# Giving out the last network's input sums earlier, and letting late weights' remainders run on two engines: one fused attention, mixture and two-layer kernel on one Trainium2 core

## The chip, the cores and the metric

The kernel runs on one core of a Trainium2 chip (trn2). The metric is device time of one execution in microseconds (us), the median of several. TensorE does the matrix products and transposes, VectorE, ScalarE and GpSimd the elementwise work, SyncE issues transfers. The profile calls them PE, DVE, ACT, POOL and SP; PEld is TensorE's weight load.

## The reference

Three stages run one after the other; all arrays are float32.

```python
# 1. attention, B=2, H=8, S=576, D=64, window 128, a linear bias by distance
attn = softmax(where(mask, q @ k.T * scale + bias, -1e9)) @ v
x = attn.transpose(0, 2, 1, 3).reshape(1152, 512)
# 2. four experts, F=1024, weighted by p = domain_probs / sum
out = sum(p[:, e:e+1] * (relu(x @ w1[e]) @ w2[e]) for e in range(4))
# 3. the last network, 512 -> 2048 -> 512
h = relu(out @ w_in)
y = (h * h) @ w_out
```

## The kernel before, in words

Each float32 operand of a product is split into a rounded high part and the remainder (low part), and three products (high by high, high by low, low by high) are accumulated. The high part is a copy on ScalarE, the remainder a subtraction on VectorE or GpSimd (`rest`, L499 to L501).

The last network is handled as two more experts, so that `e` runs from 0 to 5: 0 to 3 are the experts of stage 2, 4 and 5 the two halves of the 2048 wide hidden layer (in the code `E` is 4). For `e` from 1 on the work is a list of items `(e, ch, g)`: `ch` is one of two groups of tokens (`PAIRS`: four tiles of 128 tokens, and five), `g` one of four quarters of the 1024 hidden columns. An item has two parts. `gemm1_pair` (L1052) computes the first product of the item by a Strassen-like form of seven products of sums, 42 matmuls into three PSUM tiles (`hps`), in the order b11, t2, t1, b21, t3, b22, m4. `flush_one` (L1364) then runs the second product (`gemm2_pair`) of the item before, six matmuls for each token tile into PSUM tiles `yacc`, and at every second `g` empties them (`evac`, L1178). So TensorE's stream is product one of item n, product two of item n-1, product one of item n+1, and so on.

The sums in the first product are of two kinds. Those of the weights are made in `w_forms` (L339): four sums (`wsum`, `add`), roundings on ScalarE (`ha`, `hs`), remainders (`la`, `ls`), fifteen steps on GpSimd with the four remainders (`wl`, `w_ops`, `lo`) of the matching second weight. Those of the inputs are t1, t2, t3 and m4 (high parts `ht`, `hm`, low parts `lt`, `lm`). For the last network the inputs are the outputs of stage 2, so they are made at the turn from `e` = 3 to `e` = 4: `to_x2` (L1204) transposes the finished tiles `ytile` in pairs ("twins") on TensorE into PSUM tiles `xtp` (which share the five `yacc` slots), copies parts with ScalarE and puts a list of steps into `x2bg`: `st1`, `st2`, `sm4`, `st3`, `la` and `lb` read `xtp` in PSUM on VectorE, `hi` (ScalarE) and `lo` (VectorE or GpSimd) make the high parts and remainders. There are three pairs for `ch` = 1 (the last of a single tile) and two for `ch` = 0. The items around the turn are (3,1,2), (3,1,3), (3,0,2), (3,0,3), (4,1,0), (4,1,1), (4,0,0), (4,0,1).

What sets the order of these background steps is `fill` (L1436). It is called after each small piece of TensorE work with the time that piece takes, advances a model clock, and gives out steps whose inputs the model says are ready and whose engine the model says has room (`room`, `by`, `spare`). `x2_run` (L1303) gives out steps of `x2bg` in list order. `x2_need` (L1290) forces those of a sum just before its product. `convert` (L225) is another such list: it turns the last network's weights, which arrive as 64-bit numbers, into float32, with two half tiles in flight; four steps of VectorE (L279, L286, L293 twice) for each half. An engine executes its instructions in the order in which they were given out; an instruction that waits holds those behind it.

Lines named below: L357 `wsum` sums, L501 remainders, L1067 first product, L1078 copies p1 and p5 (ScalarE), L1082 sums u2, u3, c12, c21, c22 (VectorE), L1097 and L1092 square and relu, L1098 and L1102 high part of the hidden values, L1103 their low part for experts, L1147 second product, L1193 and L1199 emptying `yacc`, L1223 transposes, L1236 copies out of `xtp` and high parts, L1240 sums out of `xtp`.

```python
1247            end["b"] = copied(xh[:, 2:4, cb], b[:, 2:4, :], short)
1267                eng = "POOL" if clock["POOL"] <= max(clock["DVE"], clock["now"]) + 0.3 else "DVE"
1305        for _ in range(4):
1447            if conv and need and not (xbg or x2bg or x2todo) and conv_due[0] >= 1.0 and conv[0]() is not False:
```

Of the kernel before, what the change touches and what calls it, by code (L numbers as in the profile page):

```python
# [131 lines left out]
def kernel(  # L132
# [201 lines left out]

    def by(end, early=0.5):

        return clock["force"] or end <= clock["now"] + early

    def w_forms(i):  # L339
# [14 lines left out]
        def add(o, x, y, op):  # L354
            if not room("POOL"):
                return False
            nc.gpsimd.tensor_tensor(out=t["s"][:, o:o + 2, :], in0=x(), in1=y(), op=op)  # L357
            t["end"] = spent("POOL", 0.85)
# [11 lines left out]
        def part_lo(o, src):  # L370
            if not room("POOL"):
                return False
            js = slice(o, o + 2)
            rest("POOL", t["la"][0][:, js, :], src, t["ha"][0][:, js, :])
            spent("POOL", 0.85)
# [8 lines left out]
        def done(o):  # L384
            if not (by(t["hs", o // 4 * 4]) and room("POOL")):
                return False
            if o == 0:
                free.insert(0, buf)
                t["ls"] = w_tile([P, 8, P], F32R, "ls")
            js = slice(o, o + 2)  # L390
            rest("POOL", t["ls"][0][:, js, :], t["s"][:, js, :], t["hs"][0][:, js, :])
            spent("POOL", 0.85)
            if o == 6:
                w1t[e, g] = [t[x] for x in ("ha", "hs", "la", "ls")]
                free.append(t["buf"])
                ready.add(i)
# [15 lines left out]
    def w_ops(i):  # L412
# [24 lines left out]
        def lo(o):  # L437
            if not (by(held["end"]) and room("POOL")):
                return False
            cs = slice(o, o + 2 * P)  # L440
            rest("POOL", flat(held[0][1])[:, cs], raw[:, cs], flat(held[0][0])[:, cs])
            spent("POOL", 0.85)
# [609 lines left out]
    def gemm1_pair(e, ch, g):  # L1052
# [60 lines left out]
        mm(pb, s2, "t2", True, False)  # L1113
        add(u2, pb, p1)
# [8 lines left out]
        mm(pb, s3, "t3", False, False)  # L1123
        add(u3, pb, p1)
# [4 lines left out]
        mm(pc, s4, "b22", False, True)  # L1129
        add(c12, pc, u2)  # L1130
# [73 lines left out]
    def to_x2(ch, tiles):  # L1204
# [58 lines left out]
        def lo(name):  # L1263
            def go():
                if "h" + name not in end or not by(end["h" + name], 0.4):
                    return False
                eng = "POOL" if clock["POOL"] <= max(clock["DVE"], clock["now"]) + 0.3 else "DVE"
                if not room(eng):
# [5 lines left out]
        x2bg.extend([  # L1274
# [3 lines left out]
            hi("t2"),  # L1278
            hi("t1"),
            step("sm4", short, "st2", lambda us: minus(s["m4"], a[:, 2:4, :], s["t2"], us)),  # L1280
            step("st3", short, "b", lambda us: minus(s["t3"], b[:, 2:4, :], s["t3"], us)),
            hi("m4"),
            step("lb", short, "b", lambda us: minus(xl[:, 2:4, cb], b[:, 2:4, :], f32(xh[:, 2:4, cb]), us)),
            hi("t3"),
            lo("t2"), lo("t1"), lo("t3"), lo("m4"),
        ])

    x2made, x2bg = [], []
# [75 lines left out]
    def flush_one():  # L1364
# [5 lines left out]
        turning = (e, f) == (E - 1, NQ - 1)  # L1370
# [4 lines left out]
        if turning:  # L1375
# [3 lines left out]
        for i, tile_ in enumerate(tiles):  # L1379
# [56 lines left out]
    def fill(share, us, need=0.0):  # L1436
# [9 lines left out]
        for _ in range(3):  # L1446
            if conv and need and not (xbg or x2bg or x2todo) and conv_due[0] >= 1.0 and conv[0]() is not False:
# [354 lines left out]
    for it, (e, ch, f, two) in list(enumerate(items))[N1:]:  # L1802
# [69 lines left out]
```

## Time and profile before

| what | value |
| --- | --- |
| three timed runs | 677.43, 677.45, 680.63 us; median 677.45 |
| the profiled execution | 679.51 us, of which the span from first to last instruction is 677.70 |
| mean granted TensorE clock | 0.995 |
| busy: PE | 657.7 us (97%) |
| busy: DVE, POOL, ACT | 476.6, 412.4, 320.4 us |

The busy shares are means over the whole span. A stall of TensorE stands in the profile as idle time ahead of an instruction, with the engine that ended it; granted clock is given for each stretch as a share of full speed. "x3" in a row of the timeline means that three like instructions were merged into one line.

### The profile page before, as it was taken

To read this page: it belongs to the slowest core of one execution; us is meant where nothing else is said; L and a number is where in the kernel's file an instruction comes from. 1 tells how busy PE (TensorE), PEld (TensorE's weight loads), DVE (VectorE), ACT (ScalarE), POOL (GpSimd) and SP (SyncE) were. 2 spreads that over 40 slices of the span, in tenths; PEclk is the share of its full clock that TensorE was granted. 3 is DMA by queue.
4 is the path that set the end of the run, shared out by engine and by line. 5 is a ranking of instruction groups with operands and counts; after the bars stand their busy time and mean duration, and the time that the engine had idled before them with its cause. 6 is when DMAs were issued, how large, how long until landed. Compare 5 with 4: busy or idle time off the path is not lost.

```text
span 677.7 us, 11173 instructions
## 1 busy us (share of the span) xinstructions
PE 657.7 (97%) x3947; PEld 586.0 (86%) x3947; DVE 476.6 (70%) x1037; ACT 320.4 (47%) x802; POOL 412.4 (61%) x506
## 2 busy tenths in 40 slices
PE   9999999999999999999999999996989999899997
PEld 8879988899898989898998988885879898798896
DVE  6898977648888876877777777765675666445553
ACT  6998877514443343434343443453444543333220
POOL 1799967438686554557546435535566667688421
PEclk9999999999999999999999999999999999899999
DMA  9942221023214244343434343311114233000012
GB/s 239 259 139 74 74 82 40 1 63 118 100 61 135 100 135 145 111 139 116 139 115 144 125 144 111 104 48 46 63 47 156 77 95 110 0 1 1 1 63 77
DMA packets 44023, 64.44 MB, mean 95 GB/s; under 512 B 4160, under 2 KB 26176, under 8 KB 43968
## 3 DMA queue, kind: packets, MB, share of 16 engines
q1 hardware_dynamic: 32704, 39.35, 18.8%
q10 hardware_dynamic: 11264, 24.38, 11.3%
q8 instruction: 31, 0.51, 0.3%
q14 instruction: 24, 0.20, 0.1%
HBM read 52.97 MB, written 10.75 MB: 94 GB/s over the span
## 4 chain that ended last, share of the span: by engine, by line
PE 74%; POOL 13%; issue 6%; DVE 4%; ACT 2%; DMA 1%; ACTq 0%; POOLq 0%; DVEq 0%
PE yacc L1147 27%; PE hps L1067 24%; PE yacc L1173 6%; PE hps L950 6%; POOL hmem L501 4%; PE xps L735 3%; PE tp L871 2%; POOL wl L501 2%; PE sc L815 2%; POOL ls L501 2%; POOL wsum L357 1%; POOL la L501 1%; PE sc L525 1%; PE hps L1683 1%; DVE wconv L293 1%
## 5 line engine op out<-in xcount | busy, mean ns | idle before, releaser
L1147 PE MATMUL yacc<-wh,hmem 128*128 128x512 f32 x720 | 230.7, 392 | 3.7 <-DVE y L1240 3.7
L1147 PEld LDWEIGHTS yacc<-wh,hmem 128*128 128x128 f32 x720 | 136.0, 189 | 32.0 <-issue 4.5
L1147 PE MATMUL yacc<-wl,hmem 128*128 128x512 f32 x360 | 141.1, 392 | 0.0
L501 POOL TENSOR_TENSOR wl<-wraw,wh 128x256 fp32r<-128x256 f32 (+1 forms) x91 | 85.5, 964 | 36.4 <-ACT wh L434 22.0
L501 POOL TENSOR_TENSOR hmem<-c,hmem 128x320 fp32r<-128x320 f32 (+1 forms) x64 | 59.4, 941 | 64.9 <-ACT hmem L1098 64.8
L501 POOL TENSOR_TENSOR ls<-wsum,hs 128x256 fp32r<-128x256 f32 x80 | 64.4, 831 | 54.8 <-ACT hs L381 54.0
L1082 DVE TENSOR_TENSOR u<-hps,p 128x256 f32<-128x256 f32 (+1 forms) x80 | 36.5, 456 | 85.1 <-PE hps L1067 72.2
L1078 ACT ACTIVATE p<-hps 128x256 f32<-128x256 f32 (+1 forms) x80 | 32.8, 411 | 110.1 <-PE hps L1067 110.0
L1147 PEld LDWEIGHTS yacc<-wl,hmem 128*128 128x128 f32 x360 | 68.0, 189 | 12.7
L501 POOL TENSOR_TENSOR la<-wraw,ha 128x256 fp32r<-128x256 f32 x60 | 52.5, 898 | 27.1 <-ACT ha L367 27.1
L293 DVE SCALAR_TENSOR_TENSOR wconv<-wraw,wconv 128x512 int32<-128x512 int32 x64 | 56.8, 887 | 1.3
L1102 ACT ACTIVATE hmem<-c 128x256 fp32r<-128x256 f32 (+1 forms) x72 | 31.2, 445 | 53.1 <-DVE c L1082 51.5
L1098 ACT ACTIVATE hmem<-c 128x320 fp32r<-128x320 f32 (+1 forms) x64 | 27.3, 446 | 57.9 <-DVE c L1092 38.4
L1067 PE MATMUL hps<-ht,ls 128*128 128x320 f32 (+1 forms) x160 | 48.1, 301 | 2.5 <-POOL ls L501 2.5
L1103 DVE SCALAR_TENSOR_TENSOR hmem<-c,hmem 128x256 fp32r<-128x256 f32 (+1 forms) x72 | 40.2, 577 | 14.3 <-ACT hmem L1102 12.9
L1067 PE MATMUL hps<-ht,hs 128*128 128x320 f32 (+1 forms) x160 | 48.0, 300 | 0.8 <-ACT ht L1236 0.8
L1067 PE MATMUL hps<-lt,hs 128*128 128x320 f32 (+1 forms) x160 | 47.9, 299 | 0.6 <-POOL lt L501 0.6
L1067 PE MATMUL hps<-xh,ha 128*128 128x320 f32 (+1 forms) x160 | 47.7, 298 | 0.3 <-ACT p L1078 0.3
L1067 PE MATMUL hps<-xh,hs 128*128 128x320 f32 (+1 forms) x160 | 47.6, 297 | 0.5 <-DVE u L1082 0.4
L1067 PE MATMUL hps<-xh,la 128*128 128x320 f32 (+1 forms) x160 | 47.6, 297 | 0.4 <-POOL la L501 0.4
L1067 PE MATMUL hps<-xl,hs 128*128 128x320 f32 (+1 forms) x160 | 47.5, 297 | 0.0
L1067 PE MATMUL hps<-xl,ha 128*128 128x320 f32 (+1 forms) x160 | 47.4, 297 | 0.0
(148 smaller groups left out, 1723.1 us busy)
## 6 DMA issues: line engine op xcount, KB each, us to landing
wraw<-in_w_dram SPq DMA_DIRECT2D x32, 512.0 KB, 4.1
wraw<-in_w_out_dram ACTq DMA_DIRECT2D x16, 512.0 KB, 3.8
w<-wconv ACTq DMA_DIRECT2D x32, 256.0 KB, 3.9
wraw<-w SPq DMA_DIRECT2D x16, 512.0 KB, 3.3
wraw<-in_w_in_dram ACTq DMA_DIRECT2D x14, 512.0 KB, 3.7
rq<-in_qT_dram SPq DMA_DIRECT2D x8, 256.0 KB, 7.2
out_dram<-y SPq DMA_DIRECT2D x8, 256.0 KB, 2.1
rk<-in_kT_dram SPq DMA_DIRECT2D x8, 192.0 KB, 5.2
```

The lines of the kernel that those rows point to most:

```text
L293: nc.vector.scalar_tensor_tensor(out=ai, in0=raw[j][:, :, part], scalar=amount, in1=ai, op0=op, op1=ALU.bitwise_or,)
L501: e.tensor_tensor(out=out, in0=in0, in1=f32(in1), op=ALU.subtract)
L735: nc.tensor.matmul(out=xps[:, :, o0:o0 + w], lhsT=l_, rhs=r_, start=(i == 0 and l_ is wh_ and r_ is hi), stop=(i == len(mm) - 1 and l_ is ...
L950: nc.tensor.matmul(out=ps, lhsT=l_[:, k, cs], rhs=r_[:, k, cols], start=(k == 0 and r_ is xh and l_ is wh and not second), stop=(k == KT - ...
L1067: nc.tensor.matmul(out=ps, lhsT=a[l_][:, k, :], rhs=b[r_][:, k, :], start=start and k == 0 and l_ == r_, stop=stop and k == 1 and l_ == 1, ...
L1078: nc.scalar.activation(out=out, in_=x, func=ACTF.Copy)
L1082: nc.vector.tensor_tensor(out=out, in0=x, in1=y, op=ALU.add)
L1098: nc.scalar.activation(out=hh, in_=r, func=ACTF.Copy)
L1102: nc.scalar.activation(out=hh, in_=src, func=ACTF.Relu)
L1103: nc.vector.scalar_tensor_tensor(out=hl, in0=src, scalar=0.0, in1=f32(hh), op0=ALU.max, op1=ALU.subtract)
L1147: nc.tensor.matmul(out=y, lhsT=l_[:, ns], rhs=r_[:, fo, :], start=(first and fo == 0 and j == 0), stop=(last and fo == FTQ - 1 and j == 2),)
L1173: nc.tensor.matmul(out=y, lhsT=l_[:, ns], rhs=r_[:, fo, :], start=(first and j == 0), stop=(last and j == 2),)
```

## The change

It changes the order and the engine of background steps. No step is added or left out, and TensorE's instructions and SyncE's stand in the same order as before.

1. `x2_run` is called at more places: in `gemm1_pair` ahead of the sums u2, u3 and c12, and in `flush_one` ahead of `evac`; with a slack for VectorE's modelled backlog (`x2_slack`), and up to eight steps instead of four.
2. In `x2bg` the steps that read PSUM (`reads`) stand ahead of the roundings and remainders of all pairs that are still waiting.
3. `lo` chooses GpSimd only if its model clock is 0.4 behind, instead of up to 0.3 ahead.
4. `turning` is true during items (3,0,2), (3,0,3), (4,1,0) and (4,1,1). In these no step of `convert` is given out.
5. `side` lets a weight step of the last network go to VectorE if GpSimd has no room, `x2bg` is empty, `turning` is false and `spare` finds room. All of `add`, `part_lo`, `done` and `lo` use it.

```diff
+    def side(i):
+        if room("POOL"):
+            spent("POOL", 0.85)
+            return "POOL"
+        if order[i][0] >= E and not (x2bg or turning[0]) and spare(0.45):
+            return "DVE"
...
         def add(o, x, y, op):
-            if not room("POOL"):
+            if not by(t.get("end", 0.0), 1.0):
                 return False
-            nc.gpsimd.tensor_tensor(out=t["s"][:, o:o + 2, :], in0=x(), in1=y(), op=op)
-            t["end"] = spent("POOL", 0.85)
+            eng = side(i)
+            if eng is None:
+                return False
+            e_ = nc.gpsimd if eng == "POOL" else nc.vector
+            e_.tensor_tensor(out=t["s"][:, o:o + 2, :], in0=x(), in1=y(), op=op)
+            t["end"] = clock[eng]
...
         def part_lo(o, src):
-            if not room("POOL"):
+            eng = side(i)
+            if eng is None:
                 return False
             js = slice(o, o + 2)
-            rest("POOL", t["la"][0][:, js, :], src, t["ha"][0][:, js, :])
-            spent("POOL", 0.85)
+            rest(eng, t["la"][0][:, js, :], src, t["ha"][0][:, js, :])
...
         mm(pb, s2, "t2", True, False)
+        x2_run(0.9)
         add(u2, pb, p1)
...
         mm(pb, s3, "t3", False, False)
+        x2_run(0.9)
         add(u3, pb, p1)
...
         mm(pc, s4, "b22", False, True)
+        x2_run(0.7)
         add(c12, pc, u2)
...
-                if need not in end or not (room("DVE", 1.0) and by(end[need], 0.4)):
+                if need not in end or not (room("DVE", x2_slack[0]) and by(end[need], 0.4)):
...
-                eng = "POOL" if clock["POOL"] <= max(clock["DVE"], clock["now"]) + 0.3 else "DVE"
-                if not room(eng):
+                eng = "POOL" if clock["POOL"] <= max(clock["DVE"], clock["now"]) - 0.4 else "DVE"
+                if not room(eng, x2_slack[0] if eng == "DVE" else 1.2):
...
-        x2bg.extend([
+        reads = [
             step("st1", short, "a", lambda us: minus(s["t1"], b[:, 0:2, :], s["t1"], us)),
             step("la", 2 * short, "a", lambda us: minus(xl[:, :, ca], a, f32(xh[:, :, ca]), us)),
             step("st2", short, "st1", lambda us: minus(s["t2"], b[:, 2:4, :], s["t1"], us)),
-            hi("t2"),
-            hi("t1"),
+            step("st3", short, "b", lambda us: minus(s["t3"], b[:, 2:4, :], s["t3"], us)),
             step("sm4", short, "st2", lambda us: minus(s["m4"], a[:, 2:4, :], s["t2"], us)),
-            step("st3", short, "b", lambda us: minus(s["t3"], b[:, 2:4, :], s["t3"], us)),
-            hi("m4"),
             step("lb", short, "b", lambda us: minus(xl[:, 2:4, cb], b[:, 2:4, :], f32(xh[:, 2:4, cb]), us)),
-            hi("t3"),
-            lo("t2"), lo("t1"), lo("t3"), lo("m4"),
-        ])
+        ]
+        i = sum(x[0][0] not in "hl" or x[0] in ("la", "lb") for x in x2bg)
+        x2bg[i:i] = reads
+        x2bg.extend(k(x) for x in ("t2", "t1", "t3", "m4") for k in (hi, lo))
...
-    def x2_run():
+    def x2_run(slack=1.0):
-        for _ in range(4):
+        x2_slack[0] = slack
+        for _ in range(8):
...
             if last:
+                x2_run(1.1)
                 evac(e, ch, [tile_], f, two)
...
-            if conv and need and not (xbg or x2bg or x2todo) and conv_due[0] >= 1.0 and conv[0]() is not False:
+            if conv and need and not (xbg or x2bg or turning[0]) and conv_due[0] >= 1.0 and conv[0]() is not False:
...
+        turning[0] = (e, ch, f // 2) in ((E - 1, 0, 1), (E, 1, 0))
```

In `done` and in the `lo` of `w_ops` the engine is chosen in the same way as in `part_lo`. The rows that follow are instructions in the order of the program, without times; the numbers in the names count tiles. Line numbers of the changed kernel are higher by up to 18.

Place one is VectorE in item (3,0,2), from the steps ahead of its sum u2 to its sum u3 (`hps_5135` is the PSUM tile that also takes t3 and m4). Before:

```order
L279 TENSOR_SCALAR wconv_2389<-wconv_2389 128x512
L286 TENSOR_SCALAR wconv_2389<-wconv_2389 128x512
L293 SCALAR_TENSOR_TENSOR wconv_2389<-wraw64_2387,wconv_2389 128x512 x2
L1082 TENSOR_TENSOR u2_5129<-hps_5135,p1_5127 128x256
L279 TENSOR_SCALAR wconv_2389<-wconv_2389 128x512
L286 TENSOR_SCALAR wconv_2389<-wconv_2389 128x512
L293 SCALAR_TENSOR_TENSOR wconv_2389<-wraw64_2388,wconv_2389 128x512
L1103 SCALAR_TENSOR_TENSOR hmem_109<-hps_5134,hmem_109 128x256
L1082 TENSOR_TENSOR u3_5130<-hps_5135,p1_5127 128x256
```

Now:

```order
L513 TENSOR_TENSOR ls_5058<-wsum_4959,hs_4957 128x256
L279 TENSOR_SCALAR wconv_2389<-wconv_2389 128x512
L286 TENSOR_SCALAR wconv_2389<-wconv_2389 128x512
L293 SCALAR_TENSOR_TENSOR wconv_2389<-wraw64_2387,wconv_2389 128x512 x2
L1094 TENSOR_TENSOR u2_5129<-hps_5135,p1_5127 128x256
L1115 SCALAR_TENSOR_TENSOR hmem_109<-hps_5134,hmem_109 128x256
L1094 TENSOR_TENSOR u3_5130<-hps_5135,p1_5127 128x256
L1094 TENSOR_TENSOR c12_5131<-hps_5136,u2_5129 128x256
```

Three steps of `convert` between u2 and the low part of the hidden values are gone from there. Ahead of u2 there is now one remainder `ls` of a weight.

Place two is VectorE in item (4,1,0), the first of the last network, around its sum u2 (`y_2505` is the tile of the third, single pair; `lt21`, `lt11`, `lm41` and `xl` are remainders of t2, t1, m4 and t3 for `ch` = 1). Before:

```order
L1240 TENSOR_TENSOR y_2505<-xtp_5313,y_2505 128x128
L501 TENSOR_TENSOR lt21_5237<-y_2505,ht21_5236 128x2x64
L1082 TENSOR_TENSOR u2_5433<-hps_5439,p1_5431 128x320
L501 TENSOR_TENSOR lm41_5239<-y_2510,hm41_5238 128x2x128
L1240 TENSOR_TENSOR y_2505<-xtp_5313,y_2505 128x128 x2
L1240 TENSOR_TENSOR xl_84<-xtp_5313,xh_83 128x2x64
L501 TENSOR_TENSOR xl_84<-y_2505,xh_83 128x2x64
L1082 TENSOR_TENSOR u3_5434<-hps_5439,p1_5431 128x320
```

Now:

```order
L1255 TENSOR_TENSOR xl_84<-xtp_5310,xh_83 128x4x64
L1255 TENSOR_TENSOR y_2505<-xtp_5310,y_2505 128x128 x3
L1255 TENSOR_TENSOR xl_84<-xtp_5310,xh_83 128x2x64
L513 TENSOR_TENSOR xl_84<-y_2510,xh_83 128x2x128
L513 TENSOR_TENSOR lt21_5232<-y_2505,ht21_5231 128x2x64
L1094 TENSOR_TENSOR u2_5436<-hps_5442,p1_5434 128x320
L513 TENSOR_TENSOR lt11_5230<-y_2505,ht11_5229 128x2x64
L513 TENSOR_TENSOR xl_84<-y_2505,xh_83 128x2x64
L513 TENSOR_TENSOR lm41_5234<-y_2505,hm41_5233 128x2x64
L1094 TENSOR_TENSOR u3_5437<-hps_5442,p1_5434 128x320
```

The reads of `xtp_5310` now all stand ahead of u2. The remainders of t1 and of m4 for the third pair, which GpSimd made, now stand on VectorE behind u2.

Place three is GpSimd ahead of item (5,0,1): sums, remainders `la` and remainders `ls` of its weights, among the remainders of the hidden values (`hmem`) of item (5,0,0). Before:

```order
L501 TENSOR_TENSOR hmem_109<-c22_6488,hmem_109 128x256
L357 TENSOR_TENSOR wsum_6518<-wraw_6119 128x256
L501 TENSOR_TENSOR hmem_109<-c12_6486,hmem_109 128x256
L501 TENSOR_TENSOR hmem_109<-c21_6487,hmem_109 128x256
L501 TENSOR_TENSOR hmem_109<-c22_6488,hmem_109 128x256
L357 TENSOR_TENSOR wsum_6518<-wsum_6518,wraw_6119 128x256
L357 TENSOR_TENSOR wsum_6518<-wraw_6119 128x256
L357 TENSOR_TENSOR wsum_6518<-wraw_6119,wsum_6518 128x256
L501 TENSOR_TENSOR la_6517<-wraw_6119,ha_6515 128x256 x3
L501 TENSOR_TENSOR ls_6608<-wsum_6518,hs_6516 128x256 x4
```

Now:

```order
L513 TENSOR_TENSOR wl_6356<-wraw_5952,wh_6355 128x256 x2
L369 TENSOR_TENSOR wsum_6462<-wsum_6462,wraw_6115 128x256
L369 TENSOR_TENSOR wsum_6462<-wraw_6115 128x256
L513 TENSOR_TENSOR hmem_109<-c22_6497,hmem_109 128x256
L513 TENSOR_TENSOR hmem_109<-c12_6495,hmem_109 128x256
L369 TENSOR_TENSOR wsum_6462<-wraw_6115,wsum_6462 128x256
L513 TENSOR_TENSOR hmem_109<-c21_6496,hmem_109 128x256
L513 TENSOR_TENSOR hmem_109<-c22_6497,hmem_109 128x256
L513 TENSOR_TENSOR la_6461<-wraw_6115,ha_6459 128x256
L513 TENSOR_TENSOR ls_6587<-wsum_6462,hs_6460 128x256 x4
```

Between the last `hmem` step and the first `ls` step there stood three sums and three `la` steps; now one `la` step stands there. One of the sums and two `la` steps went to VectorE. Over the whole kernel VectorE makes 17 of the weight steps that GpSimd made (7 `wl`, 4 `ls`, 4 `la`, 2 `wsum`).

## Rows read from the trace of the kernel before

**Rows 1.** Part 1 of the page: busy us, share of the span, instructions.

```profile
PE 657.7 (97%) x3947; PEld 586.0 (86%) x3947; DVE 476.6 (70%) x1037; ACT 320.4 (47%) x802; POOL 412.4 (61%) x506
```

**Rows 2.** Waits of PE: line, released by, us in total, times, longest us.

```profile
PE yacc L1147 <- DVE y L1240: 3.7, 2, 2.2
PE hps L1067 <- POOL ls L501: 2.5, 2, 1.9
PE hps L1067 <- POOL lm L501: 2.1, 1, 2.1
```

**Rows 3.** Windows: busy us of PE, PEld, DVE, ACT, POOL; granted clock, DMA share, GB/s.

```profile
430.00:500.00 70.00, 61.10 (x347) 52.79 (x346) 45.98 (x94) 31.00 (x82) 38.72 (x49) 0.98 0.19 64
500.00:630.00 130.00, 126.71 (x738) 113.99 (x737) 75.92 (x137) 54.23 (x122) 95.64 (x122) 0.99 0.19 62
...
474.00:478.00 4.00, 4.00 (x12) 3.10 (x12) 2.36 (x5) 0.87 (x2) 2.57 (x4) 0.61 0.33 122
...
584.00:588.00 4.00, 4.00 (x27) 4.00 (x26) 0.84 (x3) 0.77 (x2) 0.64 (x1) 0.70 0.00 0
```

**Rows 4.** Timeline of PE: start us, us, what, idle before it and its releaser.

```profile
439.65 0.38 PE L1067 MATMUL hps<-hm,ha 128*128 128x256 f32 x1 [1.16 <-DVE u L1082]
...
460.52 0.47 PE L1147 MATMUL yacc<-wh,hmem 128*128 128x512 f32 x1 [2.21 <-DVE y L1240]
...
463.36 0.30 PE L1067 MATMUL hps<-xh,ha 128*128 128x320 f32 x1
...
465.18 0.41 PE L1067 MATMUL hps<-ht,hs 128*128 128x320 f32 x1 [0.79 <-ACT ht L1236]
...
472.87 0.42 PE L1067 MATMUL hps<-lm,ha 128*128 128x320 f32 x1 [2.09 <-POOL lm L501]
...
473.71 0.59 PE L1147 MATMUL yacc<-wh,hmem 128*128 128x512 f32 x1
...
494.50 0.47 PE L1147 MATMUL yacc<-wh,hmem 128*128 128x512 f32 x1 [1.54 <-DVE y L1240]
...
499.64 0.38 PE L1067 MATMUL hps<-lt,hs 128*128 128x256 f32 x1 [0.59 <-POOL lt L501]
...
533.27 0.39 PE L1067 MATMUL hps<-ht,ls 128*128 128x256 f32 x1 [0.62 <-POOL ls L501]
...
580.44 0.39 PE L1067 MATMUL hps<-xh,la 128*128 128x256 f32 x1 [0.37 <-POOL la L501]
...
583.31 0.58 PE L1067 MATMUL hps<-ht,ls 128*128 128x256 f32 x1 [1.90 <-POOL ls L501]
```

**Rows 5.** Chain that ended last: start us, us, an undisturbed first product.

```profile
241.95 6.15 PE hps L1067 x42
```

**Rows 6.** Timeline of DVE, columns as in rows 4, at the turn.

```profile
437.82 1.11 DVE L293 SCALAR_TENSOR_TENSOR wconv<-wraw,wconv 128x512 int32<-128x512 int32 x1
...
456.82 1.83 DVE L1103 SCALAR_TENSOR_TENSOR hmem<-c,hmem 128x256 fp32r<-128x256 f32 x2
...
459.51 1.20 DVE L1240 TENSOR_TENSOR y<-xtp,y 128x256 f32<-128x256 f32 x3
...
465.16 0.29 DVE L501 TENSOR_TENSOR lt<-y,ht 128x128 fp32r<-128x128 f32 x1 [3.40 <-ACT ht L1236]
466.61 0.49 DVE L1082 TENSOR_TENSOR u<-hps,p 128x320 f32<-128x320 f32 x1 [1.15 <-PE hps L1067]
...
492.22 0.41 DVE L501 TENSOR_TENSOR lm<-y,hm 128x256 fp32r<-128x256 f32 x1
...
494.93 0.92 DVE L501 TENSOR_TENSOR lt<-y,ht 128x256 fp32r<-128x256 f32 x1
```

**Rows 7.** Timeline of POOL, columns as in rows 4.

```profile
472.37 0.45 POOL L501 TENSOR_TENSOR lm<-y,hm 128x128 fp32r<-128x128 f32 x1
...
579.66 2.11 POOL L501 TENSOR_TENSOR la<-wraw,ha 128x256 fp32r<-128x256 f32 x3
...
581.85 2.79 POOL L501 TENSOR_TENSOR ls<-wsum,hs 128x256 fp32r<-128x256 f32 x4
```

More of the change, by code (lines that the diff above doesn't have):

```diff
@@ L384, in done @@
         def done(o):
-            if not (by(t["hs", o // 4 * 4]) and room("POOL")):
+            eng = side(i) if by(t["hs", o // 4 * 4]) else None
+            if eng is None:
                 return False
@@ L390, in done @@
             js = slice(o, o + 2)
-            rest("POOL", t["ls"][0][:, js, :], t["s"][:, js, :], t["hs"][0][:, js, :])
-            spent("POOL", 0.85)
+            rest(eng, t["ls"][0][:, js, :], t["s"][:, js, :], t["hs"][0][:, js, :])
             if o == 6:
@@ L437, in lo @@
         def lo(o):
-            if not (by(held["end"]) and room("POOL")):
+            eng = side(i) if by(held["end"]) else None
+            if eng is None:
                 return False
             cs = slice(o, o + 2 * P)
-            rest("POOL", flat(held[0][1])[:, cs], raw[:, cs], flat(held[0][0])[:, cs])
-            spent("POOL", 0.85)
+            rest(eng, flat(held[0][1])[:, cs], raw[:, cs], flat(held[0][0])[:, cs])
             if o == 2 * n - 2 * P:
@@ L1277, in to_x2 @@
             step("st2", short, "st1", lambda us: minus(s["t2"], b[:, 2:4, :], s["t1"], us)),
-            hi("t2"),
-            hi("t1"),
+            step("st3", short, "b", lambda us: minus(s["t3"], b[:, 2:4, :], s["t3"], us)),
             step("sm4", short, "st2", lambda us: minus(s["m4"], a[:, 2:4, :], s["t2"], us)),
-            step("st3", short, "b", lambda us: minus(s["t3"], b[:, 2:4, :], s["t3"], us)),
-            hi("m4"),
             step("lb", short, "b", lambda us: minus(xl[:, 2:4, cb], b[:, 2:4, :], f32(xh[:, 2:4, cb]), us)),
-            hi("t3"),
-            lo("t2"), lo("t1"), lo("t3"), lo("m4"),
-        ])
-    x2made, x2bg = [], []
+        ]
+        i = sum(x[0][0] not in "hl" or x[0] in ("la", "lb") for x in x2bg)
+        x2bg[i:i] = reads
+        x2bg.extend(k(x) for x in ("t2", "t1", "t3", "m4") for k in (hi, lo))
+    x2made, x2bg, turning = [], [], [False]
     def x2_need(name):
@@ L1301, in x2_need @@
         clock["force"] = False
-    def x2_run():
-        for _ in range(4):
+    x2_slack = [1.0]
+    def x2_run(slack=1.0):
+        x2_slack[0] = slack
+        for _ in range(8):
             for i, step in enumerate(x2bg):
@@ L1369, in flush_one @@
             first, last = f == 0, f == FT - 1
-        turning = (e, f) == (E - 1, NQ - 1)
+        ending = (e, f) == (E - 1, NQ - 1)
         if first:
@@ L1374, in flush_one @@
         tiles = ys[e, ch]
-        if turning:
+        if ending:
             c0 = PAIRS[ch][0] // P
@@ L1384, in flush_one @@
             if last:
+                x2_run(1.1)
                 evac(e, ch, [tile_], f, two)
-            if turning and i in (2, 4):
+            if ending and i in (2, 4):
                 run_x2()
```

## The prediction

> **What bounds the kernel now.** I read the busy times first: PE works 657.7 of 677.70 us [rows 1], so what can be won by another order of background steps is PE's idle time, some 20 us, and no more. Next comes the windows view [rows 3]: from 430 to 500 us PE is busy for 61.10 of 70 us, so 8.9 us of the idle time lie at the turn into the last network; from 500 to 630 it is idle for another 3.3 us. VectorE is busy for 45.98 and 75.92 us in these stretches, so it has room; what it does in front of a step that PE waits for matters, not its sum. Third, the waits of PE by releaser [rows 2]: VectorE's sums out of `xtp`, GpSimd's weight remainders `ls` and one `lm` lead. Last, the timeline gives each wait its place [rows 4]. Six of the nine waits there belong to the turn, three to weights that come late (533 to 583 us).
>
> A wait can cost more than itself. From 474 to 478 us, behind the wait that ends at 472.87, the granted clock is 0.61 with PE busy throughout; from 584 to 588 us, behind the one that ends at 583.31, it is 0.70 [rows 3, 4]. Full speed is the 2.4 GHz level, so a part of each stretch ran at 1.2 GHz. The first cost (1 - 0.61) x 4 = 1.56 us, the second 1.2 us. The mean of 0.98 over 430 to 500 us gives 1.4 us lost, about the same as that one stretch: the longer wait that ends at 460.52 cost no clock.
>
> **The turn, step by step.** TensorE's order is unchanged, so I go along its waits.
>
> *Item (3,0,2).* PE waits 1.16 us for u3, because steps of `convert` stand between u2 and u3; the last of them ran for 1.11 us from 437.82 [rows 4, 6]. Place one shows that they are gone. The `ls` step that now stands ahead of u2 costs 0.4 to 0.9 us there (below) and is covered by VectorE's wait for u2's product. Saved: 1.16.
>
> *Item (3,0,3).* Five reads now stand between its u2 and the low part ahead of u3, one of them a wide one, where four stood. A read takes 0.4 (1.20 for three [rows 6]), a wide one up to twice that. I charge 0.4, with 0 and 0.8 as ends, since some of it lies beside ScalarE's work for the same low part. Lost: 0.4.
>
> *Product two of (3,0,2).* Its third tile waits 2.21 us for a `yacc` slot that is still an `xtp` tile; the slot is free when `sm4` of the second pair has read it. Those reads start only when VectorE is through two slow `hmem` steps (1.83 from 456.82 [rows 6]). Before, four reads with a wide one came first up to and with `sm4`, about 1.9 us; now `st1` and the wide `la` are done earlier and three come, 1.2 us. The two `hmem` steps stay in front. Saved: 0.6, with 0 and 2.2 as ends.
>
> *Item (4,1,0).* Its first product runs from 463.36 to 473.71 [rows 4], 10.35 us, where the same 42 matmuls take 6.15 undisturbed [rows 5]: 4.2 us too long, of which two waits are 0.79 (for `ht` of the third pair) and 2.09 (for `lm`, which ran 0.45 us on GpSimd from 472.37, behind an `hmem` step [rows 7]). Place two shows both pulled ahead: the reads of the third pair, its `xl` and `lt21` stand ahead of u2, and `lm41` stands on VectorE. But `lt11`, which t1 needs from its second matmul on, stands behind u2, and u2 waits for the end of t2. This makes a new wait: u2 0.49, then `lt` 0.29 [rows 6], and the latency of two hand-overs, less one matmul of 0.15: about 0.9 us. Saved: 4.2 - 0.9 = 3.3, with 2.0 and 4.0 as ends.
>
> *The clock behind it.* With 2.09 us of waiting gone and at most 1.5 us in one piece left, I take the stretch from 474 as run at full speed: saved 1.56, or nothing, if the waits that are left bring the lower level all the same.
>
> *Product two of (4,1,0).* The 1.54 us ahead of 494.50 are a `yacc` slot again, and `sm4` again. After the last slow steps of the item VectorE did `lm` and `st1` (0.41 each, pitch 0.33), `la`, `st2` and `sm4`; now `la`, `st2`, `st3`, `sm4`. Saved: 0.3.
>
> *Item (4,0,0).* PE waits 0.59 us for `lt`, made by GpSimd between weight steps [rows 4]. The step is now on VectorE ahead of u2 and no longer behind weight steps. Saved: 0.59.
>
> The turn in sum: 1.16 - 0.4 + 0.6 + 3.3 + 1.56 + 0.3 + 0.59 = 7.1 us.
>
> **The late weights.** PE waits 0.62 us for `ls` of item (4,0,3), 0.37 for `la` and 1.90 for `ls` of item (5,0,1) [rows 4]. Place three is the last of these. GpSimd made three sums, three `la` (2.11 us) and then `ls` from 581.85 [rows 7], 0.70 us a step. Five of the six steps ahead of `ls` are gone from there, two or three to VectorE and the others into the pauses before and between the `hmem` steps. So `ls` can start some 5 x 0.70 = 3.5 us earlier, and 1.9 are needed. For (4,0,3) the same holds with 0.62 needed. Saved: 2.89, and the 1.2 us of clock behind them: 4.1 us.
>
> What I cost at nothing: the 17 weight steps that VectorE takes over. A remainder of this shape took 0.41 us at 492.22 and 0.92 at 494.93, where GpSimd was at work as well [rows 6], so 7 to 16 us, mostly between 500 and 630 us, where VectorE idles for 54 us [rows 3]. If that cover is gone, each such step in front of a sum u2 or u3 delays PE by up to 0.9 us. The steps of `convert` that are held back come later on VectorE, in the same cover; the weight loads stand in the same order on SP, and the last weights are needed tens of us after their conversion.
>
> The rows show one thing that speaks against this part: the same shape took 0.92 us instead of 0.41 beside GpSimd. The Trainium skill (SBUF — State Buffer, "Who interferes with whom") says that a VectorE instruction with two SBUF inputs contends with a GpSimd instruction that reads SBUF, and that the one that comes second is blocked until the first is through. The two durations agree with it. By that rule alone a moved step is no gain at all, as the two engines would only take turns, and the sum would keep the turn's 7.1 us and lose the 4.1. I side with the rows in that GpSimd has pauses ahead of `hmem` steps, and that some steps move into these.
>
> **The sum.** 7.1 + 4.1 = 11.2 us off the profiled execution's 679.51 gives 668.3. That execution is 2.06 us above the median of 677.45. If the difference is the cost of profiling, the median falls to 666.3. If the median's execution simply had no stretch at the lower clock, 2.76 us of the gain are not there to be had and it falls to 669.0. I take the middle, **667.5 us**.
>
> **The rivals.**
>
> *The waits at the turn move on, and the clock falls again.* The new wait for `lt11`, the slot waits of 1.5 and 1.2 us that I leave standing and the delay in (3,0,3) are all near each other. If each comes out at its bad end and the 1.56 us stay, the turn saves 1.2 - 0.8 + 0 + 2.0 + 0 + 0.3 + 0.6 = 3.3 instead of 7.1: 671.3 us. For it: `hmem` steps still stand ahead of both slot reads. Against it: four of the six waits lose their cause in the order. Chance 0.15.
>
> *VectorE and GpSimd only take turns.* Then late weights stay late, 4.1 us are kept: 671.6 us. This is the case of the rule above. For it: 0.92 against 0.41. Against it: the pauses. Chance 0.11.
>
> *The change does not do what it says*, because the waits are set by something behind the order (the transfers of weights, ScalarE's copies out of `xtp`): within 2 us of 677.45. Against it: the releasers in the rows are VectorE and GpSimd. Chance 0.08.
>
> *Slower.* A weight step that is put ahead of a sum u2 waits for GpSimd or ScalarE, and VectorE, in order, holds u2 behind it. GpSimd waits for `hmem` parts from ScalarE, which wait for VectorE. PE has no cover for u2: it needs the same PSUM tile again two products later. Such steps stand ahead of a sum in some eight items from 480 us on. It decides from 1.4 us a place (8 x 1.4 = 11.2); at 2 us it costs 16 against a gain of 11.2: 682 us. For it: nothing in the code waits for real events, only for a model's. Against it: VectorE waits for PE, and not PE for it, at most sums u2. Chance 0.08.
>
> **How the numbers follow.** My forecast has the remaining 0.58. With the ends of its unknown terms it spans 664 to 670.5; up to 673.5 the range takes in the next two cases, and leaves out 0.16 above and a little below. Half a per cent, 3.4 us, is about what a measurement can tell from no change. Faster by more: 0.58 + 0.15 + 0.11 = 0.84; within: 0.08; slower: 0.08.
>
> **What would show it.** In the profile after, PE is idle for less than 4 us from 430 to 490 us and has no wait for `ls` of over 0.5 us; the wait for `lm` is gone, a wait for `lt` on VectorE of 0.5 to 1.2 us stands at the start of t1 of (4,1,0), and two waits for `yacc` on VectorE of 1 to 1.6 us are left; no stretch has a granted clock below 0.9. VectorE's weight steps take 0.4 to 1 us. I am wrong if a wait of over 1 us on VectorE's u2 or u3 shows up from 500 us on, if `ls` is still waited for, or if the lower clock stays.

## The result and the profile after

The changed kernel takes **667.86 us** (median of 4 runs, 667.46 to 667.98). The kernel before, run beside it, takes 678.74 (4 runs, 677.43 to 680.63): ratio 0.984, 95% interval 0.981 to 0.987. In the later comparisons the kernel before has medians of 679.2 to 679.7 over 11 to 17 runs, so the 677.45 shown ahead of the prediction was at its low end, and the profiled execution's 679.51 was typical. The profiled execution of the changed kernel takes 667.80, of which the span is 665.7.

The busy times (part 1 of the page) answer to [rows 1]:

```profile
PE 653.3 (98%) x3947; PEld 583.1 (88%) x3947; DVE 491.9 (74%) x1056; ACT 320.9 (48%) x802; POOL 403.0 (61%) x487
```

The span is 12.0 us shorter. Of that 4.4 us are PE's busy time, with the same 3947 instructions, and 7.6 us its idle time. The windows answer to [rows 3]:

```profile
430.00:500.00 70.00, 66.58 (x393) 58.37 (x393) 51.87 (x103) 34.92 (x92) 43.14 (x53) 1.00 0.18 61
500.00:630.00 130.00, 128.52 (x760) 115.98 (x759) 91.60 (x158) 53.30 (x120) 89.27 (x108) 1.00 0.19 64
```

At the turn PE is busy for 5.5 us more of the same 70, and the granted clock is 1.00 where it was 0.98 and 0.99. The waits of PE by releaser answer to [rows 2]:

```profile
PE hps L1079 <- DVE u L1094: 2.6, 6, 0.8
PE yacc L1162 <- DVE y L1255: 1.8, 2, 1.3
...
PE hps L1079 <- DVE lt L513: 0.5, 1, 0.5
```

Waits for `ls`, `la` and `lm` are gone. What is left of 0.3 us or more from 430 us on (timeline of PE) answers to [rows 4]:

```profile
444.42 0.65 PE L1238 MATMUL xtp<-ident,y 128*128 128x128 f32 x4 [0.66 <-DVE y L1208]
...
453.79 0.38 PE L1079 MATMUL hps<-hm,ha 128*128 128x256 f32 x1 [0.37 <-DVE u L1094]
...
458.77 0.47 PE L1162 MATMUL yacc<-wh,hmem 128*128 128x512 f32 x1 [1.26 <-DVE y L1255]
...
464.35 0.41 PE L1079 MATMUL hps<-lt,hs 128*128 128x320 f32 x1 [0.53 <-DVE lt L513]
...
487.41 0.47 PE L1162 MATMUL yacc<-wh,hmem 128*128 128x512 f32 x1 [0.53 <-DVE y L1255]
...
518.09 0.39 PE L1079 MATMUL hps<-hm,ha 128*128 128x256 f32 x1 [0.51 <-DVE u L1094]
...
563.47 0.39 PE L1079 MATMUL hps<-xh,hs 128*128 128x256 f32 x1 [0.84 <-DVE u L1094]
```

New among these, beside the wait for `lt` that was forecast, are the 0.37 us at 453.79, in the place where 0.4 us were charged to item (3,0,3), and the last two, which were not forecast. What stands ahead of u2 at 563 us (timeline of VectorE) shows why:

```profile
556.31 1.97 DVE L293 SCALAR_TENSOR_TENSOR wconv<-wraw,wconv 128x512 int32<-128x512 int32 x2
558.20 1.09 DVE L513 TENSOR_TENSOR wl<-wraw,wh 128x256 fp32r<-128x256 f32 x1
559.22 0.96 DVE L369 TENSOR_TENSOR wsum<-wraw 128x256 f32<-128x256 f32 x1
560.09 0.96 DVE L279 TENSOR_SCALAR wconv<-wconv 128x512 f32<-128x512 f32 x1
561.09 0.85 DVE L286 TENSOR_SCALAR wconv<-wconv 128x512 int32<-128x512 int32 x1
561.97 1.11 DVE L293 SCALAR_TENSOR_TENSOR wconv<-wraw,wconv 128x512 int32<-128x512 int32 x1
563.00 0.41 DVE L1094 TENSOR_TENSOR u<-hps,p 128x256 f32<-128x256 f32 x1
```

Two weight steps and the steps of `convert` run back to back from 556.31 to 563.0, each 1.4 to 2.7 times as long as the shortest of its kind in this trace, and u2 comes after them. Ahead of the sum that PE waits for at 518 us stand three steps of `convert`.

### The profile page after: what moved, and what is told of

Its sections match the earlier page's. It is cut to its first block, busy times and chain, and to the rows that moved or that the text cites. A ratio compares the mean times of both kernels' runs of the same rounds, so it can differ in the third digit from the quotient of the medians.

```text
span 665.7 us, 11186 instructions
## 1 busy us (share of the span) xinstructions
PE 653.3 (98%) x3947; PEld 583.1 (88%) x3947; DVE 491.9 (74%) x1056; ACT 320.9 (48%) x802; POOL 403.0 (61%) x487
## 5 line engine op out<-in xcount | busy, mean ns | idle before, releaser
L513 POOL TENSOR_TENSOR wl<-wraw,wh 128x256 fp32r<-128x256 f32 (+1 forms) x84 | 81.3, 991 | 39.1 <-ACT wh L446 26.9
L513 POOL TENSOR_TENSOR ls<-wsum,hs 128x256 fp32r<-128x256 f32 x76 | 62.7, 851 | 54.5 <-ACT hs L393 53.7
L513 POOL TENSOR_TENSOR la<-wraw,ha 128x256 fp32r<-128x256 f32 x56 | 49.9, 913 | 22.0 <-ACT ha L379 22.0
```

Source lines behind the costliest of these rows:

```text
L513: e.tensor_tensor(out=out, in0=in0, in1=f32(in1), op=ALU.subtract)
```

## The experiments

The theory is that of the prediction: the turn's waits go because VectorE reaches their causes earlier, the late weights' because VectorE takes a share, and a long wait costs clock behind it. I call the parts of the change **reads** (early calls, new list order, new threshold; parts 1 to 3), **hold** (no `convert` during the turn; part 4) and **weights** (part 5).

**Weights undone.** `side` returns GpSimd or nothing.

```diff
             return "POOL"
-        if order[i][0] >= E and not (x2bg or turning[0]) and spare(0.45):
-            return "DVE"
```

> Weight steps on GpSimd alone again, the turn as in the changed kernel. Theory (late weights were worth 2.9 us of waits, and up to 1.2 us of clock behind the longest): waits for ls and la on GpSimd of 2 to 3 us are back between 500 and 590 us, the small waits for u of 0.5 and 0.8 us at 518 and 563 us shrink, and the time is 669.5 to 672. Rival (VectorE and GpSimd only take turns, so the moved steps won nothing): 667 to 668.5, with no wait for ls of over 0.5 us.

672.06 us (671.72 to 672.22), 0.06 over the theory's range. Waits of PE, and two windows from about the end of the first wait on:

```profile
PE hps L1077 <- POOL ls L511: 1.9, 1, 1.9
PE hps L1077 <- POOL la L511: 1.9, 1, 1.9
```

```profile
572.00:576.00 4.00, 1.60 (x9) 1.40 (x10) 0.00 (x0) 1.85 (x4) 3.92 (x7) 0.76 0.00 0
576.00:580.00 4.00, 4.00 (x20) 4.00 (x20) 0.43 (x1) 0.77 (x2) 0.69 (x2) 0.50 0.00 0
```

The weights were worth 4.2 us net in the finished kernel, and the rival (the engines only take turns) falls. Item (5,0,1) is 6.6 us longer here (the two waits, and the clock of the second window), but the small waits for u shrink: items (4,0,2) and (5,0,0) together are 1.4 us shorter. The rest of the way to 4.2 lies ahead of the turn, where this execution is 0.9 us ahead of the other. The wait for `la` is 1.9 where the kernel before had 0.37 [rows 4], in a kernel whose turn is some 8 us shorter while GpSimd has the same weight steps to do ahead of that item.

**Weights alone**: part 5 put into the kernel before, as in the diff of the change, `turning` set in the same items.

```diff
+        turning[0] = (e, ch, f // 2) in ((E - 1, 0, 1), (E, 1, 0))
         quota["n"] = pace(it)
```

> The kernel before, with weight steps allowed on VectorE and nothing else of the change. Theory: the waits of the turn stay (some 8 us of idle PE from 430 to 500 us), the waits for ls and la from 500 us on are gone, and the time is 2.5 to 4.5 us below the kernel before: 673 to 675 where that takes 677.4. The granted clock is full from 580 to 590 us. Rival (the two engines take turns): within 1 us of the kernel before. Second rival (steps in front of u2 hold PE): slower than before by 1 us or more, with waits for u on VectorE.

674.03 us, ratio 0.993 (0.991 to 0.995). The mechanism is the theory's: the waits of the turn stay, those for `ls` and `la` are gone, the clock is full from 580 to 590 us. The gain of 5.2 us on the kernel before beside it (679.22) is more than the theory's 2.5 to 4.5. Its single runs sort by mean granted clock: 671.81 us at 1.000, 673.67 to 674.32 at 0.997, 675.50 at 0.994. In the profiled execution the clock falls behind the third tile's slot wait (timeline of PE and windows):

```profile
460.06 0.47 PE L1159 MATMUL yacc<-wh,hmem 128*128 128x512 f32 x1 [2.18 <-DVE y L1252]
```

```profile
460.00:462.00 2.00, 1.94 (x7) 1.60 (x8) 1.31 (x5) 1.56 (x4) 2.00 (x4) 0.77 0.00 0
462.00:464.00 2.00, 2.00 (x6) 1.54 (x5) 0.00 (x0) 0.00 (x0) 1.25 (x2) 0.50 0.00 0
464.00:466.00 2.00, 1.51 (x8) 1.13 (x6) 0.00 (x0) 0.39 (x2) 0.00 (x0) 0.88 0.00 0
```

**Hold undone.**

```diff
-            if conv and need and not (xbg or x2bg or turning[0]) and conv_due[0] >= 1.0 and conv[0]() is not False:
+            if conv and need and not (xbg or x2bg or x2todo) and conv_due[0] >= 1.0 and conv[0]() is not False:
```

> Steps of convert are allowed during the turn again, as in the kernel before. In the program three of them stand between u2 and u3 of item (3,0,2) again, and three ahead of the emptying of yacc after item (4,1,0). Theory: a wait for u3 of about 1.2 us is back near 440 us, and the slot wait of the third tile grows from 1.26 by up to 0.7, as the wide la read falls behind the slow hmem steps: 669 to 670.5. Rival (the early reads alone made the difference): 667.5 to 668.3.

677.54 us (12 runs): the undoing costs 9.7 us, far more than either theory had. The largest part lies at the three `convert` steps that I had seen ahead of the emptying of `yacc` and had not priced. Timeline of PE, then of VectorE:

```profile
460.73 0.47 PE L1162 MATMUL yacc<-wh,hmem 128*128 128x512 f32 x1 [2.35 <-DVE xl L1255]
...
478.83 1.58 PE L1238 MATMUL xtp<-ident,y 128*128 128x128 f32 x8 [2.66 <-DVE y L1208]
...
494.69 0.47 PE L1162 MATMUL yacc<-wh,hmem 128*128 128x512 f32 x1 [3.18 <-DVE y L1255]
```

```profile
475.43 0.41 DVE L279 TENSOR_SCALAR wconv<-wconv 128x512 f32<-128x512 f32 x1
475.87 0.97 DVE L286 TENSOR_SCALAR wconv<-wconv 128x512 int32<-128x512 int32 x1
476.88 1.23 DVE L293 SCALAR_TENSOR_TENSOR wconv<-wraw,wconv 128x512 int32<-128x512 int32 x1
478.04 2.06 DVE L1208 SCALAR_TENSOR_TENSOR y<-yacc,pt,y 128x512 f32<-128x512 f32 x3
```

Earlier reads empty the list sooner; an empty list is what lets `convert` in; and 2.6 us of it then stand ahead of the emptying, which the transposes and all reads behind them wait for. Behind the wait for the transposes the clock is at 0.50 as well (windows):

```profile
480.00:482.00 2.00, 2.00 (x7) 1.61 (x7) 0.09 (x1) 1.05 (x3) 1.92 (x4) 0.50 0.04 8
```

From the product ahead of the transposes up to the first product of (4,1,1) this costs 4.2 us, and the product with the slot wait of 3.18 another 2.6, of 9.1 us between the two profiled executions. The wait for u3 (1.07 us), the slot wait of 2.35 and one of 0.78 for `ht` come on top, and item (4,0,2) gives 1.1 us back.

**Old list order**: `reads` and its insertion replaced by the list of the kernel before.

```diff
-        i = sum(x[0][0] not in "hl" or x[0] in ("la", "lb") for x in x2bg)
-        x2bg[i:i] = reads
-        x2bg.extend(k(x) for x in ("t2", "t1", "t3", "m4") for k in (hi, lo))
+        x2bg.extend([
+            step("st1", short, "a", lambda us: minus(s["t1"], b[:, 0:2, :], s["t1"], us)),
...
```

> The steps of each pair stand in the old list order (roundings and remainders of the pair between its reads, no reads of a later pair ahead), all else as in the changed kernel. In the program the remainder lm of the third pair then stands behind the square of c12 in item (4,1,0), and t1's remainder is on GpSimd. Theory: a wait for lm of 1 to 2 us is back near 468 us, sm4 ahead of st3 shortens two slot waits by 0.3 each: 668.5 to 670 at full clock, up to 671.5 if the lower clock comes back behind the wait. Rival (the list order is nothing, since each sum is forced before its product): 667 to 668.3.

671.25 us: 3.4 us more, and a miss in part. The theory had up to 671.5 only with the lower clock behind the wait; no stretch of the profiled execution has it while PE works, and the five runs at a mean clock of 0.999 or 1.000 take 670.19 to 671.85, where 668.5 to 670 was expected. One of the two slot waits got longer, not shorter (1.53 for 0.53). PE waits again for `lm`, which stands behind the square of c12, as expected:

```profile
470.18 0.41 PE L1079 MATMUL hps<-lm,ha 128*128 128x320 f32 x1 [1.83 <-DVE lm L513]
```

**Hold alone**, in the kernel before, with `turning` set as above.

```diff
-            if conv and need and not (xbg or x2bg or x2todo) and conv_due[0] >= 1.0 and conv[0]() is not False:
+            if conv and need and not (xbg or x2bg or turning[0]) and conv_due[0] >= 1.0 and conv[0]() is not False:
```

> The kernel before, with convert held back during the turn and nothing else of the change. Theory (the hold matters because earlier reads empty the list and let convert in; alone it only takes away the wait for u3 of 1.16 us): 676 to 678.3 where the kernel before has a median of 679.2; the slot waits of 2.2 and 1.5 us and the wait for lm of 2.1 us stay. Rival (the hold is the turn's whole gain, since undoing it alone cost 9.7 us): 670 to 673.

683.61 us, ratio 1.0065 (1.0047 to 1.0084): slower than before; neither theory had it. The wait for u3 is gone, but the wait for `la` ahead of (5,0,1) grows from 0.37 to 1.86, the waits for `ls` from 2.5 to 3.2 in sum, and the slot wait at the second product of (4,1,0) from 1.54 to 2.19 (timeline of PE), with a lower clock behind it that the kernel before did not have (windows):

```profile
491.92 0.77 PE L1147 MATMUL yacc<-wh,hmem 128*128 128x512 f32 x1 [2.19 <-DVE xl L1240]
...
582.33 0.39 PE L1067 MATMUL hps<-xh,la 128*128 128x256 f32 x1 [1.86 <-POOL la L501]
```

```profile
492.00:494.00 2.00, 2.00 (x5) 1.62 (x6) 2.00 (x7) 1.68 (x4) 2.00 (x4) 0.50 0.00 0
```

The held steps are caught up later, and in the code a call of `fill` that gives out a step of `convert` gives out no weight step; that this is what makes the weights late was not tried by itself.

**Planted waits.**

```diff
         x2_run(0.9)
+        for _ in range(DOSE.get((e, ch, g), 0)):
+            add(u3, pb, p1)
         add(u2, pb, p1)
```

> The changed kernel with 6, 9, 9 and 12 copies of the sum u3 made on VectorE ahead of u2 in items (1,0,2), (1,1,3), (2,0,2) and (3,0,0), which hold u2 and with it TensorE: waits for u of about 1.0, 1.8, 2.0 and 3.0 us, 7.8 in sum, in stretches that have the full clock without them. Theory (a wait of about 2 us or more costs its own length and then a stretch at the lower clock of 1.5 to 2 us, a shorter one only itself): two or three stretches with a granted clock near 0.5 behind the longer waits, none behind the first; 678 to 681.5, and single runs that differ by a stretch's cost. Rival (a wait costs its own length alone, the low stretches in the kernel before belong to the turn): 675 to 676.5, granted clock 1.0 in these stretches.

687.21 us; the profiled execution 688.65. The planted waits came out longer than meant (12.93 us in sum instead of 7.8), so the time is beyond the theory's range too. Timeline of PE, and a window of 6 us behind each:

```profile
223.20 0.39 PE L1081 MATMUL hps<-xh,hs 128*128 128x256 f32 x1 [1.77 <-DVE u L1096]
...
261.77 0.63 PE L1081 MATMUL hps<-xh,hs 128*128 128x320 f32 x1 [3.49 <-DVE u L1096]
...
327.18 0.39 PE L1081 MATMUL hps<-xh,hs 128*128 128x256 f32 x1 [3.15 <-DVE u L1096]
...
380.72 0.58 PE L1081 MATMUL hps<-xh,hs 128*128 128x256 f32 x1 [4.52 <-DVE u L1096]
```

```profile
223.00:229.00 6.00, 5.80 (x34) 5.18 (x35) 4.49 (x9) 2.08 (x5) 3.66 (x5) 1.00 0.00 0
262.00:268.00 6.00, 6.00 (x23) 5.77 (x24) 2.48 (x6) 0.97 (x3) 0.00 (x0) 0.57 0.03 8
328.00:334.00 6.00, 6.00 (x28) 5.22 (x27) 4.90 (x9) 2.07 (x5) 2.49 (x3) 0.72 0.01 3
381.00:387.00 6.00, 6.00 (x25) 5.53 (x26) 3.26 (x7) 2.46 (x6) 1.84 (x3) 0.53 0.00 0
```

Behind the last three the clock falls to the 1.2 GHz level with PE busy throughout; (1 - 0.57) x 6, (1 - 0.72) x 6 and (1 - 0.53) x 6 are 2.6, 1.7 and 2.8 us. Together with the waits that is 20.0 of the 20.85 us by which this execution is longer. The first, of 1.77 us, brought none. The rival falls.

**Short waits only**: the same, with five copies in each of ten items.

```diff
-    DOSE = {(1, 0, 2): 6, (1, 1, 3): 9, (2, 0, 2): 9, (3, 0, 0): 12}
+    DOSE = {(e, 0, g): 5 for e in (1, 2, 3) for g in range(4) if (e, g) < (3, 2)}
```

> The changed kernel with 5 copies of the sum u3 on VectorE ahead of u2 in ten items of 256 columns, (1,0,0) to (3,0,1). By the last planted doses (1.77 us at 6 copies, 3.15 at 9, 4.52 at 12: 0.46 a copy) each holds TensorE for about 1.3 us, 13 us in sum, as much as the four waits of 1.77 to 4.52 us together, which took the time to 687.2 (688.65 in the profiled execution). Theory (only a long wait brings the lower level behind it): no stretch with a granted clock below 0.9, 680 to 682. Rival (the lower level follows the sum of waiting): stretches near 0.5 again, 685 or more.

700.29 us, far over the theory's range; the rival had set no upper bound, and stretches near 0.50 are there. But the run does not test the sum: two waits for p1 (4.8 us) and late weights (`la` 3.0, `ls` 1.5) came on top, since the planted steps pushed other work back. Its rows do bear on the question: behind the nine waits of 1.32 us and behind one of 1.94 the clock stays at 1.00; it falls behind the first planted one, which came out at 2.55, and behind the late weights and the second wait for p1 (2.87). Nine waits of 1.32 us, 11.9 us in sum, without a lower clock speak against the rival.

**The look at the need taken out of the weights.**

```diff
-        if order[i][0] >= E and not (x2bg or turning[0]) and spare(0.45):
+        if order[i][0] >= E and not (x2bg or turning[0]) and room("DVE"):
+            spent("DVE", 0.45)
             return "DVE"
```

> The changed kernel, but a weight step may go to VectorE whenever the model finds VectorE less than 1.2 us ahead, without the look at how soon the next sum is needed; 13 steps go there instead of 17. Theory (a weight step in front of u2 or u3 holds TensorE, and the look at the need is what keeps that small): the waits for u grow from 2.6 to over 4 us in sum, 669 to 672. Rival (steps on VectorE have cover anywhere): 667.5 to 668.5.

669.13 us (668.58 to 669.30), waits for u of 3.7 us in sum, the longest 1.0. The look at the need is worth about 1.3 us; the time is at the low end of the theory's range, the waits a little below its 4 us.

**Hold and weights without reads; reads alone.** The first is the kernel with weights alone and the line of the hold; the second the kernel with weights undone and the hold undone as above.

```diff
-            if conv and need and not (xbg or x2bg or x2todo) and conv_due[0] >= 1.0 and conv[0]() is not False:
+            if conv and need and not (xbg or x2bg or turning[0]) and conv_due[0] >= 1.0 and conv[0]() is not False:
```

> The kernel before with the hold on convert and the weight steps on either engine, without the early calls, the new list order and the new threshold. Theory (the hold moves the wide read and others of xtp behind the slow hmem steps unless the reads are given out early, so its harm of 4.3 us stays and the weights take about 5 off): 677 to 679.5, slot waits of about 2 us on reads of xl. Rival (the harm of the hold alone was late weights, which the second engine cures): 672 to 674, no wait on reads of xl over 1 us.

> The early calls, the new list order and the new threshold alone: convert is not held back, weight steps stay on GpSimd. Theory (early reads empty the list, convert comes in at the turn, ahead of the emptying of yacc among others, as it did with the weight steps in place): slower than the kernel before by 2 to 5 us, 681 to 684, with a wait of over 2 us for the transposes near 478 us. Rival (the early reads are the turn's gain and the hold a detail): 672 to 675.

675.98 us and 679.54 us. The first lies between theory and rival: both slot waits are on reads of `xl` (2.02 and 2.20 us), as the theory had it, but the weights were worth 7.6 us against the hold alone. The second is no gain, but no loss of 2 to 5 us either, as the theory had it; the wait for the transposes (2.7 us) and the slot wait of 3.2 are there, and of the late weights only one wait for `ls` (1.9 us) is left in its trace. Now all eight combinations have a median:

| | hold off | hold on |
| --- | --- | --- |
| neither reads nor weights | 679.2 to 679.7 (before) | 683.61 |
| reads | 679.54 | 672.06 |
| weights | 674.03 | 675.98 |
| reads and weights | 677.54 | 667.86 (the change) |

No part has a worth of its own: the hold costs 4.3 us alone and 2.0 beside the weights, and gains 7.5 beside the reads and 9.7 beside both; reads gain nothing alone, cost 3.5 us beside the weights and gain 8.1 with the rest (675.98 to 667.86); weights gain between 2.0 and 7.6. Reads and hold taken as a pair do have one: 7.2 us without the weights (to 672.06) and 6.2 with them (674.03 to 667.86).

**A version that beats both kernels.** `sm4` stands ahead of `st3` and need not wait in the model for `st2` on the same engine, reads stand ahead of the slow `hmem` or square steps, and the forms of t1 ahead of u2.

```diff
+        if (e, g) == (E, 0):
+            x2_need("t1")
         x2_run(0.9)
         add(u2, pb, p1)
...
         add(c22, u3, p5)
+        x2_run(3.0)
         relu(1, 0, c21)
...
-                if need not in end or not (room("DVE", x2_slack[0]) and by(end[need], 0.4)):
+                if need not in end or not (room("DVE", x2_slack[0]) and by(end[need], 9.0 if need in ("st1", "st2") else 0.4)):
...
+            step("sm4", short, "st2", lambda us: minus(s["m4"], a[:, 2:4, :], s["t2"], us)),
             step("st3", short, "b", lambda us: minus(s["t3"], b[:, 2:4, :], s["t3"], us)),
-            step("sm4", short, "st2", lambda us: minus(s["m4"], a[:, 2:4, :], s["t2"], us)),
```

> Meant to beat the changed kernel: sm4 stands ahead of st3, the reads that release a slot stand ahead of the two slow hmem or square steps at the end of the items at the turn, and the remainder of t1 stands ahead of u2 in item (4,1,0). Theory (what is left at the turn are these waits): the slot wait of 1.26 us falls below 0.3, the wait of 0.53 for lt goes; the slot wait of 0.53 before the second product of (4,1,0) goes or stays: 666.0 to 667.0. Rival (what stands behind comes late instead: hmem steps late for the product after, or u2 late behind lt): 667.5 or more, with a wait for hmem or u in their place.

**664.56 us** (663.90 to 664.92), ratio 0.978 (0.977 to 0.980): 3.3 us below the change, more than the theory had. Its waits of PE:

```profile
PE hps L1079 <- DVE u L1094: 1.5, 4, 0.4
...
PE hps L1079 <- POOL ls L513: 0.9, 2, 0.8
...
PE yacc L1165 <- DVE y L1258: 0.2, 1, 0.2
```

The slot waits fall from 1.8 to 0.2, `lt` goes, and the first product of (4,1,0) takes the undisturbed 6.15 us.

## Why the prediction was right, and where it was not

The lengths of the parts of TensorE's stream, from first matmul to the next part's first in the two traces, against the terms of the sum:

| part | before, after | change | predicted |
| --- | --- | --- | --- |
| (3,0,2), first product | 6.45, 5.11 | -1.34 | -1.16 |
| (3,0,3), first product (both pieces) | 5.45, 5.80 | +0.35 | +0.4 |
| product two of (3,0,2) | 7.94, 6.97 | -0.97 | -0.6 |
| (4,1,0), first product | 10.35, 7.12 | -3.23 | -3.3 |
| product two of (3,0,3) behind it (clock) | 5.70, 4.34 | -1.36 | -1.56 |
| product two of (4,1,0) | 8.65, 7.64 | -1.01 | -0.3 |
| (4,0,0), first product | 5.93, 5.09 | -0.84 | -0.59 |
| (4,0,3), first product | 5.96, 5.08 | -0.88 | -0.62 |
| (5,0,1), first product | 9.20, 5.10 | -4.10 | -3.5 |
| (4,0,2) and (5,0,0), first products | 10.52, 12.36 | +1.84 | 0 |

The rows sum to -11.5 us of the span's -12.0. The mechanisms came out in their places. The sizes were helped by luck: the nine priced rows gave 13.4 us where 11.2 were predicted, and the last row, put at nothing, took most of the difference back. The new wait for the remainder of t1 is 0.53 us plus its hand-overs: the item is 0.97 over the undisturbed 6.15, and 0.9 was predicted. `lm` and `ls` are no longer waited for, no stretch of the turn or behind it has a lower clock while PE works, and PE idles 3.4 us from 430 to 490 (56.58 busy of 60). So the rival of waits that move on and bring the clock down again did not come, and the change does what it says.

**Mis-sized: the slot wait of (4,1,0)**, predicted to stay at 1.2 us and measured at 0.53: I saved one short step where the item in fact gave 0.7 us more; the reads there take `la`, `st2`, `st3` and `sm4` in 1.7 us behind the squares, with no remainder among them.

**Wrong: the moved steps costed at nothing.** VectorE's idle 54 us did not cover all of them and the later `convert` steps: (4,0,2) and (5,0,0) are 1.84 us longer, each behind a wait for a sum u. Without the moved weight steps (first experiment) the two take 10.94 us, so 1.4 of the 1.84 go with these. This is the mechanism of the slower rival, with waits of 0.5 and 0.8 us in two places instead of 2 us in eight. Taking out the look at the need made it worse by 1.3 us.

**Wrong: the held steps of `convert` costed at nothing.** The hold alone costs 4.3 us, and 2.0 beside the weights: "the same cover" does not take the steps up. The forecast did not have to pay this because the reads came with the hold, beside which it gains 7.5 us; no term of the sum said so, and that is luck as well. The two parts that the prediction added do nearly add up: the turn (reads and hold) is worth 6.2 to 7.2 us where 7.1 was predicted, the weights beside or without it 4.2 to 5.2 where 4.1 was. Inside the turn the parts do not add.

**The rule on shared access.** The Trainium skill (SBUF — State Buffer, "Who interferes with whom") has a VectorE instruction with two SBUF inputs contend with a GpSimd instruction that reads SBUF, and the second of the two wait. The durations agree: on VectorE a `wsum` took 0.41 us at 580.72, where GpSimd was idle for two thirds of it, and 0.96 at 559.22, where GpSimd was at work all the time; GpSimd's own `wl` rose from 762 to 818 ns (means from 500 to 630 us).

```profile
580.72 0.41 DVE L369 TENSOR_TENSOR wsum<-wraw 128x256 f32<-128x256 f32 x1
```

The forecast by that rule alone (671.6) is refuted by the result together with the first experiment, whose kernel needs 672.06 without the moved steps. The prediction's own reason, GpSimd's pauses, covers at most six of the 17 moved steps: these took 0.41 to 0.43 us, the other eleven 0.7 to 1.1 us, most of them with GpSimd at work throughout. They paid all the same: GpSimd's own steps grew by only some 0.05 us, and it had 17 fewer of them. That this is the whole reason was not tested.

**Profiled execution and median.** The sum gave 668.3 against the profiled execution; it took 667.80. The step down to 667.5 rested on a median of three runs that later proved low; profiling cost nothing that shows.

## What to carry to other kernels

Price a step that is held back by where it is caught up and by what it then displaces, and ask which condition a faster part makes true (here: an empty list let another list in). Test parts in combination; undoing one part and doing it alone can differ in sign, as the hold did. In an engine that executes in order, the steps that free a slot should stand ahead of those that nobody waits for yet; the three small moves in the last version gave 3.3 us.

## What the runs showed of the hardware

The price of a wait of TensorE is not its length alone. In the traces above, no single wait of up to 1.83 us was followed by a lower granted clock than 1.00. From 1.90 to 3.2 us it went either way. Waits of 1.90 (with reads alone), 1.94, 2.02, 2.21 [rows 3, 4], 2.35, 2.67 and, with the hold undone, 3.18 us brought nothing; waits of 1.90 [rows 3, 4], 2.09, 2.18 to 2.20, 2.55, 2.66, 2.87, 3.15 and, with reads alone, 3.19 were followed by a stretch near 0.50, which is the 1.2 GHz level. Single waits of 3.49 and 4.52 us both were. The same wait can do either: the third tile's slot wait brought nothing in the kernel before (2.21 us), and with weights alone (2.18 us) the granted clock was 0.77, 0.50 and 0.88 in the three windows of 2 us from 460. What decides it these runs do not show.

That goes with the spread of single runs. The 17 runs of the kernel before beside the first four experiments go from 677.17 us at a mean granted clock of 0.997 to 681.01 at 0.992; the four of the change, whose longest wait after 430 us is 1.26, stay within 0.52 us. It is no rule: the kernel with weights undone, which has a stretch at 0.50 in its trace, stays within 0.50 us too, and the one with the old list, which has none, within 2.07. A wait shortened from 2 us to 1 can give back more than 1 us: at item (4,1,0) the waits of 2.09 and 0.79 gave way to one of 0.53, and the part behind the item, then at full clock, took 1.36 us less.
